# Loads of the first weights moved to another queue, and KV plus W2's first event put side by side, in a gated two-branch attention kernel

## The chip, the cores and the metric

The kernel runs on one core of one Trainium2 chip. The metric is device time in microseconds (us) of one execution. Before the change it is 473.68 us (median of three runs, 473.68 to 473.99).

Names used here: PE is TensorE, PEld its weight loads, ACT is ScalarE, DVE is VectorE, SP is SyncE. "SPq" and "ACTq" lines are DMA issues by those engines. The profiled span is about 1.72 us shorter than the timed value of the same run.

## The reference, cut to what matters

```python
# S = 2048 tokens, D = 1024, 32 heads of 32; x, all weights and the output are bf16
def _A_ref(x, wqkv, wo):                      # linear attention
    q, k, v = split_heads(x @ wqkv)
    phi = lambda t: jnp.where(t > 0, t + 1, jnp.exp(t)) + 1e-6
    pq, pk = phi(q), phi(k)
    kv = jnp.einsum("bhsd,bhse->bhde", pk, v)
    z = jnp.einsum("bhsd->bhd", pk)
    num = jnp.einsum("bhqd,bhde->bhqe", pq, kv)
    den = jnp.einsum("bhqd,bhd->bhq", pq, z)[..., None] + 1e-6
    return merge_heads(num / den) @ wo
# _B_ref: attention of each token to 8 tokens, 2 apart (not touched here)
g = sigmoid((x * gate_w).sum(-1, keepdims=True))
return g * a + (1 - g) * b
```

## The kernel before

Two places matter. The first is the start. K of branch A is projected first: pk = phi(x @ Wk). The contraction over D = 1024 is cut into four pieces k = 0..3 of 256. For each piece the kernel needs x transposed (`xT`, by a transposing DMA) and two halves h of Wk (`WkA[h]`, 256 KB each per piece). TensorE works through piece k with 16 matmuls: eight for half 0 and eight for half 1, over the first four token tiles. While the first data are on their way, 37 matmuls on constants keep TensorE busy, which is meant to bring its clock up early.

```python
    def load_xT(k, t0, t1):
        nc.sync.dma_start_transpose(out=xT[:, 2 * k:2 * k + 2, t0 * P:t1 * P],
                                    in_=rows(x, t0 * P, t1 * P)[:, 2 * k * P:(2 * k + 2) * P])

    def load_wk(eng, k, h):
        eng.dma_start(out=WkA[h][:, 2 * k:2 * k + 2, :], in_=A_wqkv[...])        # 256 KB
    ...
    with tc.manual_schedule(engines={SP, mybir.EngineType.Activation}):
        load_wk(nc.scalar, 0, 0)
        first_act = consts.tile([P, 1], BF16, name="first_act")
        nc.scalar.activation(out=first_act[:], in_=ones[:, 0:1], func=ACT.Exp)
        load_wk(nc.scalar, 0, 1)          # half 1 of piece 0, on ScalarE's queue
        load_xT(0, 0, 2)                  # piece 0 of x, first part (token tiles 0, 1)
        load_xT(0, 2, 4)                  # second part (token tiles 2, 3)
        for k in range(1, 4):
            load_wk(nc.sync, k, 0)
            load_xT(k, 0, 4)
            load_wk(nc.sync, k, 1)
    ...
            warm_up(37)
            for k in range(4):
                for half in range(2):
                    for t in range(4):
                        for kt in (2 * k, 2 * k + 1):
                            project(first[4 * half + t], t, kt, half)
                        ...
```

The second place lies about 116 us in. KV (64-column tiles of the array) is followed by V's projection (full array), into which four "W2 events" are interleaved. Each event multiplies KV into the output weights with sixteen 32x32 tiles of the array at once.

```python
            for g in range(2):
                kvp = ps_1.tile([P, 4, 64], F32, name="kv_ps", tag="p1")
                ...                                            # 64 matmuls
                nc.vector.tensor_copy(out=KVT[:, 4 * g:4 * g + 4, :], in_=kvp[:])
            ...
            def w2_event(g, half):
                def go():
                    w2p = [ps_1.tile([P, 512], F32, name="w2_ps", tag="p1") for _ in range(4)]
                    ...                                        # 16 matmuls, 32x32 tiles, then 4 evacuations
            ...
            units = [u for t in range(4) for u in v_units(t)]
            interleave(units, [(8 + 12 * (2 * g + half), w2_event(g, half)) for g in range(2) for half in range(2)])
```

`ps_1` and `ps_pj` (the projections) have four PSUM banks each.

The softmax here doesn't subtract the row's maximum and nothing guards it: scores larger than these inputs give would overflow.

## Time and profile before

| reading | value |
|---|---|
| time, median | 473.68 us |
| profiled span | 472.3 us |
| PE busy | 466.0 us, 99% |
| PE idle for the first x piece | 0.6 us |
| first real matmul | 5.56 us |
| x's piece k=1 lands | 7.76 us |
| 17th real matmul (the first of piece 1) | 9.42 us |
| clock rises to full | 6.41 us |
| KV's first matmul to the last W2 event | 13.161 us |

The page's first lines and the shares of the chain that ended last (kernel before):

```profile
span 472.3 us, 13144 instructions
...
PE 466.0 (99%) x5734; PEld 244.7 (52%) x5765; DVE 277.4 (59%) x601; ACT 169.1 (36%) x273; POOL 15.4 (3%) x30
...
PE 98%; DMA 1%; issue 0%; ACT 0%
```

TensorE bounds the kernel, and it almost never waits. The list of waits of PE in the kernel before (engine, line and tile, what it waited for, us in total, times, longest):

```profile
PE warm L175 <- PEq L628: 0.8, 1, 0.8
PE pk_ps L169 <- DMA xT<-in_A_x_dram: 0.6, 1, 0.6
PE p_ps L295 <- issue: 0.3, 2, 0.2
```

The start of the kernel before, first PE's timeline, then SyncE's and ScalarE's DMA issues (start, duration, engine, line, operation, tiles, count, idle time before):

```profile
0.84 4.11 PE L175 MATMUL warm<-const-bfloat16-1.0 128*128 128x128 bf16 x37 [0.84 <-PEq L628]
5.56 10.72 PE L169 MATMUL pk_ps<-WkA,xT 128*128 128x512 bf16 x46 [0.61 <-DMA xT<-in_A_x_dram]
...
0.83 0.96 ACTq L98 DMA_DIRECT2D WkA<-in_A_wqkv_dram  x2
...
0.80 2.60 SPq L94 DMA_TRANSPOSE xT<-in_A_x_dram  x2
3.44 0.58 SPq L98 DMA_DIRECT2D WkA<-in_A_wqkv_dram  x1
4.08 1.24 SPq L94 DMA_TRANSPOSE xT<-in_A_x_dram  x1
```

Both halves of the first weights go out on ScalarE's queue at 0.83 to 1.79 us. SyncE issues its two transposes of x at the same time, and each occupies it for about 1.3 us. A matmul of 512 columns starts every 0.216 us at full clock and every 0.43 us before the clock rises.

The same stretch in windows of 1.5 us, kernel before (window, length, busy us of each engine, granted clock, mean busy share of the 16 DMA engines, GB/s; the share can pass 1 because packets overlap):

```profile
2.00:3.50 1.50, 1.50 (x17) 1.50 (x16) 0.00 (x0) 0.28 (x2) 0.00 (x0) 1.00 0.90 232
3.50:5.00 1.50, 1.44 (x14) 1.17 (x11) 0.00 (x0) 0.00 (x0) 0.00 (x0) 1.00 1.16 288
5.00:6.50 1.50, 0.94 (x3) 0.40 (x4) 0.00 (x0) 0.00 (x0) 0.00 (x0) 1.00 1.04 252
```

(The clock column says 1.00 from the beginning; it fills in what has no record. Whether the clock is up is read from the spacing of the matmuls and from the clock records.)

The second place, PE's timeline in the kernel before:

```profile
116.57 2.21 PE L240 MATMUL kv_ps<-G,WvA 128*64 128x64 bf16 x128
118.72 1.90 PE L295 MATMUL p_ps<-WvB,xT 128*128 128x512 bf16 x7
120.55 0.43 PE L283 MATMUL w_ps<-WoA,KVT 32*32 32x512 bf16 x16
120.91 2.76 PE L295 MATMUL p_ps<-WvB,xT 128*128 128x512 bf16 x12
```

A W2 event costs PE 0.46 us: from one V matmul to the next across it 0.677 us pass (120.236 to 120.913), less the usual 0.216.

### The profile page before, as it was taken

The numbers are of one execution on the slowest core, as the hardware profiler recorded it, in microseconds if no ns is written. First come the engines' busy times: TensorE is split into PE (matmuls) and PEld (weight loads), VectorE is DVE, ScalarE is ACT, GpSimd is POOL, SyncE is SP. The second block draws the span as 40 slices with busy tenths as digits, with TensorE's granted clock in tenths as the row PEclk, the third lists the DMA queues.
The fourth block names the chain that finished last, engine by engine and source line by source line (L and its number), as shares of the span: only waits on it lengthen the run. The fifth ranks groups of instructions, "written<-read, shape, count | busy, mean of one in ns | idle before, by whom it ended". The sixth has DMA issues, their size and how long they took to land.

```text
span 472.3 us, 13144 instructions
## 1 busy us (share of the span) xinstructions
PE 466.0 (99%) x5734; PEld 244.7 (52%) x5765; DVE 277.4 (59%) x601; ACT 169.1 (36%) x273; POOL 15.4 (3%) x30
## 2 busy tenths in 40 slices
PE   8999999999999999999999999999999999999997
PEld 5444444445444444445666666666664444444444
DVE  0496689990329999999567676767560049800000
ACT  1343321102443333333555555555551134221122
POOL 3300000500000000000000000000000000000000
PEclk9999999999999999999999999999999999999999
DMA  8999970000634233527326526452563933211001
GB/s 212 212 242 374 348 239 0 0 1 0 203 123 125 95 141 129 156 96 247 107 54 108 105 53 95 100 95 51 92 158 79 196 97 78 71 53 46 34 33 46
DMA packets 98780, 55.40 MB, mean 117 GB/s; under 512 B 70178, under 2 KB 90658, under 8 KB 98722
## 3 DMA queue, kind: packets, MB, share of 16 engines
q1 hardware_dynamic: 93282, 49.84, 41.1%
q10 hardware_dynamic: 5440, 4.72, 3.0%
q8 instruction: 45, 0.74, 0.7%
q14 instruction: 13, 0.11, 0.1%
HBM read 26.10 MB, written 15.86 MB: 89 GB/s over the span
## 4 chain that ended last, share of the span: by engine, by line
PE 98%; DMA 1%; issue 0%; ACT 0%
PE q_ps L388 27%; PE d_ps L585 12%; PE pk_ps L169 12%; PE p_ps L295 12%; PE g_ps L220 12%; PE e_ps L585 11%; PE p_ps L331 9%; PE po L467 2%; PE s2b L445 2%; DMA xT<-in_A_x_dram 1%; PE kv_ps L240 0%; PE w_ps L283 0%; ACT osb L590 0%
## 5 line engine op out<-in xcount | busy, mean ns | idle before, releaser
L388 PE MATMUL q_ps<-xT,WqB 64*64 64x512 bf16 x1024 | 68.3, 377 | 0.0
L388 PE MATMUL q_ps<-xT,WkB 64*64 64x512 bf16 x1024 | 67.9, 377 | 0.0
L156 DVE TENSOR_SCALAR e<-e 128x512 f32<-128x512 f32 x64 | 27.0, 423 | 64.3 <-ACT e L155 64.3
L295 PE MATMUL p_ps<-WvB,xT 128*128 128x512 bf16 x250 | 57.3, 379 | 0.5 <-issue 0.3
L169 PE MATMUL pk_ps<-WkA,xT 128*128 128x512 bf16 x251 | 55.6, 381 | 0.9 <-DMA xT<-in_A_x_dram 0.6
L220 PE MATMUL g_ps<-pk,xrow 128*128 128x512 bf16 x251 | 55.2, 379 | 0.3
L450 ACT ACTIVATE PT<-s2b 128x928 bf16<-128x928 f32 (+4 forms) x40 | 34.2, 854 | 45.5 <-PE s2b L445 45.5
L452 DVE TENSOR_TENSOR PT<-PT,mask 128x928 bf16<-128x928 bf16 (+4 forms) x40 | 23.6, 590 | 38.2 <-ACT PT L450 38.2
L331 PE MATMUL p_ps<-WqA,xT 128*128 128x512 bf16 x187 | 43.1, 379 | 0.3
L585 PEld LDWEIGHTS <-pqT 128*128 128x128 bf16 x272 | 26.0, 98 | 29.8 <-issue 0.4
L585 PEld LDWEIGHTS <-OBT 128*128 128x128 bf16 x272 | 26.0, 98 | 29.3
L169 PEld LDWEIGHTS <-xT 128*128 128x128 bf16 x256 | 25.1, 98 | 31.2 <-DMA xT<-in_A_x_dram 0.9
L220 PEld LDWEIGHTS <-xrow 128*128 128x128 bf16 x256 | 25.0, 98 | 30.2
L295 PEld LDWEIGHTS <-xT 128*128 128x128 bf16 x256 | 24.6, 98 | 30.0 <-issue 0.9
L388 PEld LDWEIGHTS <-WkB 64*64 64x64 bf16 x1024 | 31.7, 107 | 15.4 <-issue 0.4
L388 PEld LDWEIGHTS <-WqB 64*64 64x64 bf16 x1024 | 31.4, 106 | 15.4 <-issue 0.7
L155 ACT ACTIVATE e<-pk_ps 128x512 f32<-128x512 f32 x32 | 18.9, 597 | 40.8 <-PE pk_ps L169 36.6
L300 ACT CAST tmp<-p_ps 128x512 bf16<-128x512 f32 x32 | 18.8, 590 | 37.9 <-PE p_ps L295 29.2
L585 PE MATMUL d_ps<-WoA,pqT 128*128 128x512 bf16 (+1 forms) x133 | 30.7, 369 | 0.2
L585 PE MATMUL d_ps<-WoB,OBT 128*128 128x512 bf16 (+1 forms) x134 | 30.7, 369 | 0.1
L331 PEld LDWEIGHTS <-xT 128*128 128x128 bf16 x192 | 18.8, 98 | 22.7
L585 PE MATMUL e_ps<-WoB,OBT 128*128 128x512 bf16 (+2 forms) x133 | 29.7, 363 | 0.2
(62 smaller groups left out, 484.6 us busy)
## 6 DMA issues: line engine op xcount, KB each, us to landing
vd<-tmp SPq DMA_DIRECT2D x16, 264.0 KB
xrow<-in_A_x_dram SPq DMA_DIRECT2D x4, 1024.0 KB
out_dram<-osb ACTq DMA_DIRECT2D x31, 128.0 KB
pqd<-tmp SPq DMA_DIRECT2D x12, 256.0 KB
WvA<-in_A_wqkv_dram SPq DMA_DIRECT2D x2, 1024.0 KB
WoA<-in_A_wo_dram SPq DMA_DIRECT2D x2, 1024.0 KB
WvB<-in_B_wqkv_dram SPq DMA_DIRECT2D x2, 1024.0 KB
WqA<-in_A_wqkv_dram SPq DMA_DIRECT2D x2, 1024.0 KB
```

The source lines that it names most:

```text
L155: nc.scalar.activation(out=e[:], in_=pj[:], func=ACT.Exp)
L156: nc.vector.tensor_scalar(out=e[:], in0=e[:], scalar1=1.0, scalar2=1e-6, op0=ALU.min, op1=ALU.add)
L169: nc.tensor.matmul(pj[:], lhsT=xT[:, kt, t * P:(t + 1) * P], rhs=WkA[half][:, kt, :], start=(kt == 0), stop=(kt == KT - 1))
L220: nc.tensor.matmul(pj[:], lhsT=xrow[:, t, kt * P:(kt + 1) * P], rhs=pk[:, t, half * 512:(half + 1) * 512], start=(t == 0), stop=(t == NB - 1))
L295: nc.tensor.matmul(st["pj"][:], lhsT=xT[:, kt, t * P:(t + 1) * P], rhs=WvB[half][:, kt, :], start=(kt == 0), stop=(kt == KT - 1))
L300: nc.scalar.copy(out=v[:, half * 16:(half + 1) * 16, 0:Dh], in_=st["pj"][:].rearrange("p (h e) -> p h e", h=16))
L331: nc.tensor.matmul(st["pj"][:], lhsT=xT[:, kt, t * P:(t + 1) * P], rhs=WqA[half][:, kt, :], start=(kt == 0), stop=(kt == KT - 1))
L388: nc.tensor.matmul(banks[o][64 * j:64 * j + 64, :], lhsT=lhsT(r, kt, j), rhs=rhs(r, kt), start=first and kt == 0, stop=kt == KT - 1, skip_ ...
L445: nc.tensor.matmul(s2b[64 * par:64 * par + 64, pair, :, o:o + w], lhsT=kts[c][r, par, k0:k0 + 64], rhs=qz[r, :, par, q0 % 512:q0 % 512 + w ...
L450: nc.scalar.activation(out=pt[:, :, 0:W_], in_=s2b[:].rearrange("p a b s -> p (a b) s")[:, :, 0:W_], func=ACT.Exp, scale=SCALE)
L452: nc.vector.tensor_tensor(out=pt[:, :, 0:W_], in0=pt[:, :, 0:W_], in1=mask[:, None, base:base + W_].broadcast_to([P, 4, W_]), op=ALU.mult)
L585: nc.tensor.matmul(st["ps"][:, 0:n], lhsT=lhsT, rhs=W[c0 // 512][:, c, c0 % 512:c0 % 512 + n], start=(side == 0 and c == 0), stop=(side == ...
```

## The change

Its intent was to get the first x piece to TensorE earlier by taking half 1's weights out of ScalarE's queue, and to save one change of tile shape by putting W2's first event straight behind KV.

```diff
-    with tc.manual_schedule(engines={SP, mybir.EngineType.Activation}):
+    with tc.manual_schedule(engines={SP}):
         load_wk(nc.scalar, 0, 0)
-        first_act = consts.tile([P, 1], BF16, name="first_act")
-        nc.scalar.activation(out=first_act[:], in_=ones[:, 0:1], func=ACT.Exp)
-        load_wk(nc.scalar, 0, 1)
         load_xT(0, 0, 2)
         load_xT(0, 2, 4)
+        load_wk(nc.sync, 0, 1)
         for k in range(1, 4):
             load_wk(nc.sync, k, 0)
             load_xT(k, 0, 4)
...
-                kvp = ps_1.tile([P, 4, 64], F32, name="kv_ps", tag="p1")
+                kvp = ps_pj.tile([P, 512], F32, name="kv_ps", tag="pj")[:, 0:256].rearrange("p (c d) -> p c d", c=4)
...
-                nc.vector.tensor_copy(out=KVT[:, 4 * g:4 * g + 4, :], in_=kvp[:])
+                nc.vector.tensor_copy(out=KVT[:, 4 * g:4 * g + 4, :], in_=kvp)
...
-            interleave(units, [(8 + 12 * (2 * g + half), w2_event(g, half)) for g in range(2) for half in range(2)])
+            w2_event(0, 0)()
+            interleave(units, [(20, w2_event(0, 1)), (32, w2_event(1, 0)), (44, w2_event(1, 1))])
```

## The prediction

> **What bounds it now.** TensorE: the page has PE busy 466.0 of 472.3 us (99%), the chain of waits is 98% PE. The waits view gives PE one wait for another unit: 0.6 us for the first x piece, before the first real matmul. So the change can pay only at the start (0 to 9 us) and where PE changes tile shape (116 to 131 us).
>
> **Start.** By the packet records half 0's weights (256 KB, ScalarE's queue) land at 3.88 us. The first x transpose's packets run from 2.8 to 3.7 us, yet its completion writes go out only at 4.42, when half 1's weights (256 KB, also ScalarE's queue, 3.5 to 4.4 us) are through, and it lands at 5.51. The second x piece's completion writes follow its last packet at once (4.88) and land 0.9 us later. So half 1's weights hold back x by about 0.7 us, and x's second piece too. This agrees with the Trainium skill, "DMA: Bandwidth & Descriptors", section "Issuing engines are not separate DMA queues": both queues share the same 16 engines.
>
> With these weights out of the way I estimate completion writes at 3.75 and landing at 4.65 to 4.75, so that the first matmul follows the last warm-up matmul (start 4.63) without a gap: at 4.75, not 5.56. But the clock rises only at 6.4 us (matmul starts 5.56, 5.96, 6.39, then every 0.216). If it still does, the earlier start wins two slow matmuls: the fifth starts at 6.45 instead of 6.83, a gain of 0.4 us (0.8 if the clock rises earlier too).
>
> Half 1's weights now land at about 6.2 to 6.7 and are needed by the ninth matmul at about 7.3. Later SyncE issues slip by 0.58 us; the slack is larger (x's k=1 piece landed at 7.76, so at most 8.35, needed at 9.0). Dropping the dummy activation (0.20 us) costs nothing: the table load stays, ScalarE idles until 17 us.
>
> **KV and W2.** Each W2 event costs PE 0.46 us (V matmul starts 120.24 to 120.91, less one pitch of 0.216), though its 16 parallel tiles need one pitch: the rest is change of tile shape. The Trainium skill, "TensorEngine Tiling (Array Packing)", "Key Properties", says a mode change drains the engine. With W2's first event behind KV, KV to V (0.13) plus V to W2 (0.09 over a pitch) becomes one KV to W2 change, estimated 0.13: gain 0.1 us. By the build it waits only for the first KV copy, which ends at 118.23, before KV's last matmul at 118.59. KV in the projection banks frees the four W2 banks; without that W2 would wait for KV's second copy (119.25).
>
> **Time.** 473.68 - 0.4 - 0.1 = 473.2 us. Range 472.5 to 473.8. Faster by over 2%: 0.01; within 2%: 0.98; slower by over 2%: 0.01.
>
> **What would show it.** First x piece lands at about 4.7; PE's wait for it vanishes; first real matmul at 4.75, the first four at 0.43 each; the ninth does not wait. V starts at about 119.08 less the start's gain, and KV, W2 and the first eight V matmuls together are 0.1 shorter. Everything later is shifted by 0.5 us.
>
> **What would make it wrong.** Half 1's weights landing after 7.3 us; the clock rising at another phase (0.4 us either way); x's landing bounded by something else; a KV to W2 change as dear as the two it replaces; the timer, whose three readings differ by 0.31 us.

## The result, and the profile after

The changed kernel took 473.73 us (median of 6 runs, 473.44 to 474.22), the kernel before 473.68 (6 runs, 473.36 to 473.99). The ratio is 1.0003 with a 95% interval of 0.999 to 1.0015: no change that the timer resolves. Ratios and intervals here are those over fast runs in the same rounds; they are not quite the ratios of the medians, nor always those of the means of all runs. The forecast gain of 0.5 us did not come.

The page of the changed kernel:

```profile
span 472.5 us, 13174 instructions
...
PE 467.8 (99%) x5765; PEld 246.4 (52%) x5765; DVE 277.2 (59%) x601; ACT 169.2 (36%) x272; POOL 15.3 (3%) x30
...
PE 97%; DMA 1%; SPq 1%; ACT 0%; issue 0%
```

(PE's busy time is higher by 1.8 us, most likely because this trace has 31 more matmul records; a few per cent can be missing. The program has as many matmuls as before.) SPq is new in the chain. The waits of PE in the changed kernel:

```profile
PE pk_ps L167 <- DMA xT<-in_A_x_dram: 0.9, 2, 0.7
PE warm L173 <- PEq L627: 0.8, 1, 0.8
```

The wait for x did not vanish: it went from 0.6 us once to 0.9 us in two places. Where they are is in the timelines of the start, changed kernel, PE first and then the DMA issues:

```profile
0.84 4.11 PE L173 MATMUL warm<-const-bfloat16-1.0 128*128 128x128 bf16 x37 [0.84 <-PEq L627]
4.74 1.10 PE L167 MATMUL pk_ps<-WkA,xT 128*128 128x512 bf16 x4
6.01 2.80 PE L167 MATMUL pk_ps<-WkA,xT 128*128 128x512 bf16 x12 [0.18 <-DMA xT<-in_A_x_dram]
9.51 6.87 PE L167 MATMUL pk_ps<-WkA,xT 128*128 128x512 bf16 x31 [0.69 <-DMA xT<-in_A_x_dram]
...
0.83 0.44 ACTq L98 DMA_DIRECT2D WkA<-in_A_wqkv_dram  x1
...
0.80 2.60 SPq L94 DMA_TRANSPOSE xT<-in_A_x_dram  x2
3.45 1.09 SPq L98 DMA_DIRECT2D WkA<-in_A_wqkv_dram  x2
4.58 1.24 SPq L94 DMA_TRANSPOSE xT<-in_A_x_dram  x1
```

The first matmul starts at 4.74 us, as forecast. But after four matmuls PE waits for x's second part (landed 5.97), and after sixteen it waits for x's piece k=1, which lands at 9.46 us where it landed at 7.76 before. The 17th matmul starts at 9.51 us, after 9.42 before. The 0.8 us won at the first matmul were all given back within sixteen matmuls.

The windows of the changed kernel show what the DMA engines did meanwhile:

```profile
2.00:3.50 1.50, 1.50 (x17) 1.50 (x16) 0.00 (x0) 0.08 (x1) 0.00 (x0) 1.00 0.91 238
3.50:5.00 1.50, 1.50 (x15) 1.34 (x14) 0.00 (x0) 0.00 (x0) 0.00 (x0) 1.00 0.66 125
5.00:6.50 1.50, 1.32 (x7) 0.45 (x6) 0.00 (x0) 0.00 (x0) 0.00 (x0) 1.00 0.91 240
```

From 3.5 to 5 us they moved 125 GB/s in place of 288, at a busy share of 0.66 in place of 1.16. Summed over the packet records, 641 KB had been moved by 5.5 us, and 890 KB in the kernel before. The difference is about the 256 KB of half 1's weights, which ScalarE's queue had brought in by then.

The second place, changed kernel:

```profile
116.66 2.21 PE L238 MATMUL kv_ps<-G,WvA 128*64 128x64 bf16 x128
118.81 0.43 PE L281 MATMUL w_ps<-WoA,KVT 32*32 32x512 bf16 x16
119.18 4.49 PE L293 MATMUL p_ps<-WvB,xT 128*128 128x512 bf16 x20
```

KV to the last W2 event takes 13.054 us, after 13.161: 0.107 us saved, as forecast.

The rest of the span splits cleanly. From the 17th matmul to KV's first matmul both kernels take 107.15 us (to 0.01). Between W2 and the stage of branch B's projections (64x64 tiles) they take the same, and so they do after that stage. In that stage itself the changed kernel took 141.088 us and the kernel before 140.864. So the profiled span of the changed kernel is longer by 0.085 (start) minus 0.107 (W2) plus 0.224 (stage B), together 0.20, against 472.505 less 472.286, 0.22. The 0.22 in stage B are not an effect of the change: the next two profiles of the same changed kernel have 140.884 there. They come from one moment at which the two interleaved row streams of 64x64 matmuls shift against each other (at 352.1 us here, at 304.5 us in w2_only below). It happened in 2 of the 16 profiles. Why it happens is not settled.

### The profile page after: what moved, and what is told of

Same layout as the page of the kernel before. It is cut to its first block, busy times and chain, and to the rows that moved or that the text cites. A ratio compares the mean times of both kernels' runs of the same rounds, so it can differ in the third digit from the quotient of the medians.

```text
span 472.5 us, 13174 instructions
## 1 busy us (share of the span) xinstructions
PE 467.8 (99%) x5765; PEld 246.4 (52%) x5765; DVE 277.2 (59%) x601; ACT 169.2 (36%) x272; POOL 15.3 (3%) x30
## 4 chain that ended last, share of the span: by engine, by line
PE 97%; DMA 1%; SPq 1%; ACT 0%; issue 0%
PE q_ps L387 27%; PE d_ps L584 12%; PE p_ps L293 12%; PE g_ps L218 12%; PE e_ps L584 12%; PE pk_ps L167 11%; PE p_ps L329 9%; PE po L466 2%; PE s2b L444 2%; DMA xT<-in_A_x_dram 1%; SPq L94 1%; PE kv_ps L238 0%; PE w_ps L281 0%; SPq L98 0%; ACT osb L589 0%
## 5 line engine op out<-in xcount | busy, mean ns | idle before, releaser
L584 PE MATMUL e_ps<-WoA,pqT 128*128 128x512 bf16 (+2 forms) x136 | 30.0, 363 | 0.0
```

The lines of the kernel that those rows point to most:

```text
L584: nc.tensor.matmul(st["ps"][:, 0:n], lhsT=lhsT, rhs=W[c0 // 512][:, c, c0 % 512:c0 % 512 + n], start=(side == 0 and c == 0), stop=(side == ...
```

## The experiments

The theory (A): x's piece k=1 is the new limit, because half 1's weights now stand ahead of it in the same queue. Rivals: (B) the slow landing was chance; (C) the moment of the clock's rise, which differs from run to run, hid the gain. Within A there are two versions: A1, DMA engine time was lost while only SyncE's queue fed the engines; A2, only the place in the queue counts, by its issue time or its bytes.

The "17th matmul" of the table is read back from KV's first matmul (107.15 us later in all profiles but one, to 0.01). The exception is h1_two_issues, where the count back gives 9.36, but the 17th matmul itself starts at 8.88; there the 25th then waits for half 1's weights of piece 1 (landed 10.99, PE idle 0.25 us). "Moved" is the sum of the packet records that ended by 5.5 us, rounded down.

| run | first matmul | x k=1 lands | 17th matmul | clock rises | moved by 5.5 us | KV to last W2 | span |
|---|---|---|---|---|---|---|---|
| before | 5.56 | 7.76 | 9.42 | 6.41 | 890 KB | 13.161 | 472.29 |
| changed | 4.74 | 9.46 | 9.51 | 4.88 | 641 | 13.054 | 472.50 |
| same_again | 4.52 | 8.93 | 8.98 | 4.24 | 642 | 13.055 | 471.77 |
| same_again_2 | 4.75 | 8.85 | 8.90 | 4.85 | 636 | 13.054 | 471.69 |
| start_only | 4.77 | 9.14 | 9.20 | 5.71 | 683 | 13.161 | 472.09 |
| w2_only | 5.79 | 7.77 | 9.25 | 4.05 | 844 | 13.054 | 472.31 |
| kv_banks_only | 5.65 | 7.80 | 10.92 | 9.36 | 893 | 13.161 | 473.82 |
| w2_first_old_banks | 5.49 | 7.64 | 9.35 | 6.34 | 919 | 13.639 | 472.70 |
| x1_before_h1 | 4.74 | 6.71 | 10.47 | 6.64 | 653 | 13.055 | 473.25 |
| h1_gated_5 | 4.74 | 8.91 | 9.61 | 4.81 | 687 | 13.055 | 472.39 |
| h1_gated_1 | 4.51 | 9.42 | 12.01 | 4.13 | 605 | 13.055 | 474.81 |
| h1_between | 4.74 | 8.90 | 9.00 | 5.43 | 796 | 13.054 | 471.77 |
| h1_two_issues | 4.65 | 8.83 | 8.88 | 3.54 | 685 | 13.054 | 472.24 |
| h1_half_bytes | 5.29 | 8.40 | 8.82 | 5.47 | 681 | 13.055 | 471.60 |
| x0_whole | 4.75 | 8.58 | 8.63 | 4.80 | 771 | 13.055 | 471.33 |
| x0_whole_2 | 4.81 | 8.69 | 8.74 | 4.08 | 799 | 13.055 | 471.46 |

### same_again and same_again_2: the changed kernel, unchanged

> The changed kernel once more, unchanged. Theory A (x's k=1 piece is now the limit: its issue comes 0.5 us later and it queues behind half 1's weights in the one SyncE queue): it lands again at 9.3 to 9.6 us and the 17th matmul starts right after it at about 9.5, whatever the moment at which the clock rises. Rival B (the slow stretch of the transpose packets at 7.4 to 8.6 us was chance): it lands at about 8.4 and the 17th matmul starts by 9.1. Rival C (only the moment of the clock's rise differs from run to run, and hid the gain): the rise lies elsewhere than 4.88 us and the 17th matmul's start moves with it. Time like before's within 0.1%.

> The changed kernel a third time, beside the two above: x's k=1 piece at 8.9 to 9.5 us, 17th matmul 0.05 us behind it; ratio to before 0.999 to 1.000.

x's piece k=1 landed at 8.93 and 8.85 us, after 9.46 in the first profile: between the 9.3 to 9.6 expected under A and the 8.4 under B. The landing does differ by half a microsecond from run to run, so the first trace showed a bad case. But it never comes near the 8.35 us that the prediction gave as the latest, and the 17th matmul starts 0.05 us behind it in all three profiles. Rival B explains about 0.6 of the 1.7 us, not the rest. Rival C fails for the changed kernel: the clock rose at 4.88, 4.24 and 4.85 us, early each time, and the gain that an early rise should have brought (0.8 us) did not show. Another wait also appears: half 1's weights land at 6.9 to 7.0 and the ninth matmul waits for them. PE's waits in same_again:

```profile
PE pk_ps L167 <- DMA WkA<-in_A_wqkv_dram: 0.5, 1, 0.5
```

Times: 473.51 us (6 runs) against 473.70 before, ratio 0.999 (0.9972 to 1.0008), and 473.45 (5 runs) against 473.58, ratio 1.0002 (0.9988 to 1.0015). Neither interval excludes 1.

### start_only and w2_only: each part alone

The changed kernel with the KV and W2 lines of before, and the kernel before with only those lines changed.

> Only the change of the first loads; KV and W2 as before. Theory A: first matmul at 4.74 us, 17th at about 9.5 behind x's k=1 piece, nothing gained: 473.7 to 473.9 us (ratio 1.000 to 1.001). Rival B or C: 17th at 8.7 to 9.1, 473.2 to 473.4.

> Only KV in the projection banks and W2's first event behind it; first loads as before. All theories: first KV matmul to ninth V matmul takes 4.25 us where the kernel before takes 4.35 (0.09 less), start as before (x's k=1 piece lands at about 7.8, no wait at the 17th matmul). Time 0.1 us below before, which the timer may not resolve (ratio 0.9995 to 1.0005).

The new start alone gives a 17th matmul at 9.20 us, right behind x's piece k=1 (9.14; again between the 9.5 of A and the 8.7 to 9.1 of B or C), and 473.74 us against 473.70, ratio 0.9993 (0.9977 to 1.0009): nothing that the timer resolves. The W2 part alone gives 13.054 us from KV to the last event, 0.107 less than before, and the start is that of before. Its time, 473.90 us (ratio 1.0001, 0.9983 to 1.002), is no lower than before; its profile has the shift in stage B (141.152 against 140.864 us), which hides the 0.107. The effect of the W2 part is therefore taken from the trace, where all profiles with the same order and banks of KV and W2 agree to 0.001 us, and not from the timer.

w2_only also shows what the old start does when the clock rises early (4.05 us): the first matmul starts at 5.79, no later one waits for DMA, and the 17th follows at 9.25. With the late rise of the first profile (6.41) it was 9.42. So the old start at its usual clock ends at 9.25 to 9.42 us (kv_banks_only, 10.92, is left out; see the rare slow executions), and the new one at 8.90 to 9.51. The gain left is 0.1 to 0.3 us on average, with an overlap of the two ranges.

### kv_banks_only and w2_first_old_banks: which half of the W2 part does it

```diff
 kv_banks_only:       KV in ps_pj as in the changed kernel; W2 events at 8, 20, 32, 44 as before
 w2_first_old_banks:  KV in ps_1 as before; W2's first event straight behind KV
```

> The kernel before with KV in the projection banks, W2's first event still after eight V matmuls. First KV matmul to last W2 event's start 13.16 us as before: the banks alone give nothing, the 0.107 us come from the dropped change of tile shape.

> The kernel before with W2's first event straight behind KV, but KV still in W2's own banks. Two of the event's four banks are then KV's, and its third matmul waits for KV's second copy: a stall of about 0.5 us on PE behind KV; first KV matmul to last W2 event's start 13.4 to 13.7 us (before 13.16, with both parts 13.05).

Each was run once, for its trace; the state of a single run is unknown, so only times inside the stage are used. The banks alone change nothing (13.161). The order alone costs 0.48 us (13.639), because two of the event's four banks are still KV's. PE's timeline in w2_first_old_banks:

```profile
118.65 0.39 PE L283 MATMUL w_ps<-WoA,KVT 32*32 32x512 bf16 x3
119.24 0.43 PE L283 MATMUL w_ps<-WoA,KVT 32*32 32x512 bf16 x13 [0.20 <-DVE KVT L242]
```

Three matmuls go (two were expected), then the event waits for DVE's second copy out of KV. Only both together save the 0.107 us.

### x1_before_h1: the queue's order turned round

In the diff the loop's pass for k = 1 is written out; in the kernel the loop runs over k = 2, 3.

```diff
         load_xT(0, 2, 4)
+        load_xT(1, 0, 4)
         load_wk(nc.sync, 0, 1)
         load_wk(nc.sync, 1, 0)
-        load_xT(1, 0, 4)
         load_wk(nc.sync, 1, 1)
```

> The changed kernel with x's k=1 piece issued on SyncE ahead of half 1's first weights (order: x k=0 in two parts, x k=1, half 1 k=0, half 0 k=1, half 1 k=1). Theory A (whichever of these is last holds the matmuls up; the bytes are the same): x's k=1 piece lands at about 7.2, half 1's weights at about 8.2 to 8.6, so the stall moves to the ninth matmul (about 8.4 in place of 7.0), 17th at about 10.1, slower than the changed kernel by 0.6 to 0.9 us. If SyncE's order doesn't matter, nothing moves.

x's piece k=1 lands at 6.71 us, 2.1 to 2.8 us earlier than in the changed kernel, and half 1's weights at 8.71. The stall moves to the ninth matmul. PE's timeline in x1_before_h1:

```profile
4.74 2.83 PE L170 MATMUL pk_ps<-WkA,xT 128*128 128x512 bf16 x8
8.75 3.61 PE L170 MATMUL pk_ps<-WkA,xT 128*128 128x512 bf16 x15 [1.18 <-DMA WkA<-in_A_wqkv_dram]
```

The 17th matmul is at 10.47 us and the time 474.97 us, ratio to before 1.0027 (1.0014 to 1.0039). The direction is that of theory A: the load put behind the other holds the matmuls up. The size is larger than expected (17th at about 10.1, 0.6 to 0.9 us slower than the changed kernel): the median is 1.2 us above that of the changed kernel's first runs (473.73).

### h1_gated_5 and h1_gated_1: half 1's weights on ScalarE's queue, but later

If the old arrangement was only too early, holding half 1's weights back on ScalarE's queue should give both gains. The load is held by activations that write into its tile first.

```diff
         load_wk(nc.scalar, 0, 0)
+        for i in range(5):                       # h1_gated_1: range(1)
+            nc.scalar.activation(out=WkA[1][:, 0, 0:P], in_=ones, func=ACT.Exp)
+        load_wk(nc.scalar, 0, 1)
         load_xT(0, 0, 2)
         load_xT(0, 2, 4)
-        load_wk(nc.sync, 0, 1)
```

> The changed kernel, but half 1's first weights go back to ScalarE's queue, held there by five short activations that write into their tile first (results overwritten by the load), so that they are issued at about 3.4 us instead of 1.35. SyncE's order is that of before. Theory A: first x piece lands at 4.7 as in the changed kernel, half 1's weights at about 6.5, x's k=1 piece at 7.8 to 8.3 as it is issued 0.5 us earlier and shares the engines with a second queue; 17th matmul at 8.4 to 8.9 without a wait for DMA; 0.5 to 0.9 us faster than the changed kernel (ratio to before 0.998 to 0.999). Rival B or C: no better than the changed kernel by more than the clock's moment explains.

> As h1_gated_5 with one activation as the gate in place of five, so that half 1's weights are issued at about 2.4 us and move at about 3.5 to 4.6. Theory A1 (what was lost is engine time: while SyncE issues its transposes, one queue leaves the engines part idle, and in the kernel before half 1's weights from the other queue filled that time): first x piece lands at 4.7 to 4.9, half 1's weights at about 5.5, x's k=1 piece at 7.7 to 8.2 although nothing but the moment of one load differs from h1_gated_5 (8.91); 17th matmul at 8.3 to 9.0, ratio to before 0.998 to 0.9995. Theory A2 (only the place in SyncE's queue counts): x's k=1 piece at about 8.9 as in h1_gated_5, whose SyncE order is the same; ratio 1.000.

Both failed. With five activations the load was issued at 3.79 us (expected 3.4) and landed at 7.83 (expected 6.5), so the ninth matmul waited until 7.88; x's piece k=1 landed at 8.91 although SyncE issued it as early as in the kernel before. Time 474.27 us, ratio 1.0004 (0.9988 to 1.0021). With one activation the load was issued at 2.43 to 2.83, in the middle of SyncE's second transpose (2.15 to 3.39), and both slowed to a trickle: that part of x landed at 7.90, half 1's weights at 7.70. PE stood still for 2.4 us, and its clock fell (records: up at 4.13, down at 7.55, up at 10.96 us). The profile is of the slowest of the five runs (476.52, mean clock 0.996); the others, 474.62 to 475.58 at 0.999 to 1.000, are slow without such a fall. PE's timeline in h1_gated_1:

```profile
4.51 1.04 PE L169 MATMUL pk_ps<-WkA,xT 128*128 128x512 bf16 x4
7.95 6.39 PE L169 MATMUL pk_ps<-WkA,xT 128*128 128x512 bf16 x21 [2.39 <-DMA xT<-in_A_x_dram]
```

Time 475.12 us, ratio 1.0025 (1.0011 to 1.0039). So A1 in the simple form "fill the idle time from the other queue" is not confirmed: from 3.5 to 5 us the engines moved 106 GB/s in h1_gated_1, less even than the 125 of the changed kernel. In the kernel before the same two queues were issued together from 0.8 us and reached 288 GB/s. What makes the difference between those two overlaps is open.

### h1_two_issues and h1_half_bytes: issue time or bytes

h1_two_issues loads half 1's first 256 KB by two loads of 128 KB in place of one. h1_half_bytes makes only the first of these two loads and sets the rest of the tile to zero, so its weights are wrong. Each was timed twice: 473.74 us, ratio 0.9998 (0.9973 to 1.0024), and 472.95 us, ratio 0.9982 (0.9956 to 1.0008).

> The changed kernel with half 1's first 256 KB loaded by two SyncE loads of 128 KB in place of one: one more issue (about 0.5 us), the same bytes. If SyncE's issue time holds x's k=1 piece back: it lands 0.4 to 0.6 us later than in the changed kernel (9.3 to 9.9, changed kernel 8.85 to 9.46 in three profiles). If the bytes ahead of it do: no later than 9.5, within the changed kernel's range.

> The changed kernel with only half of half 1's first weights loaded (128 KB; the rest of the tile is set to zero, so the result is wrong on purpose): as many issues, half the bytes. If the bytes hold x's k=1 piece back (about 300 KB per us moved): it lands at 8.3 to 8.8, about 0.45 us earlier; if issue time does: 8.85 to 9.46 as in the changed kernel.

With one more issue x's piece k=1 was issued 0.45 us later (5.03 against 4.58) and landed at 8.83, no later than in the changed kernel. With half the bytes it landed at 8.40, earlier than in all four profiles of the new start (8.85 to 9.46), though in that run even the first piece landed late (5.24). One profile each, against a scatter of 0.6 us, is not much, but both say the same: bytes ahead of it delay that piece, and one extra issue at that place does not. The packet records agree. In every profile with this order of loads and all bytes, x's piece k=1 lands 0.56 to 0.81 us after the moment at which 1,328 KB have been moved (the five loads of 256 KB up to and with this piece, and 48 KB from before the first of them). That moment is 6.95 to 7.21 us in the four profiles with the old start, and 8.13 to 8.68 in the four of the new.

### h1_between: half 1's weights between the two parts of x's piece 0

```diff
         load_xT(0, 0, 2)
+        load_wk(nc.sync, 0, 1)
         load_xT(0, 2, 4)
-        load_wk(nc.sync, 0, 1)
```

> The changed kernel with half 1's weights on SyncE between the two parts of x's k=0 piece, so that they move while the second part is being issued. Theory A: first part lands at 4.7, half 1's weights at 5.3 to 5.8, second part at 6.0 to 6.4 (fifth matmul waits up to 0.4 us), kilobytes moved by 5.5 us above 750, x's k=1 piece at 8.0 to 8.5 as the engines idle less; 17th matmul at 8.5 to 9.1; 0.2 to 0.6 us faster than the changed kernel. Rival: x's k=1 piece at about 9 as the bytes ahead of it are the same.

The early part came as expected: weights at 5.70, second part of x at 6.36 us, 796 KB moved by 5.5 us. But x's piece k=1 landed at 8.90, no earlier (8.0 to 8.5 was expected; the rival, "at about 9 as the bytes ahead of it are the same", is what came); the 112 to 160 KB won by 5.5 us were lost again by 8.2. The packet records show where: the weights just ahead of that piece took from 5.29 to 7.47 us to move, as late an end as in the new start (7.10 to 7.67). The 17th matmul started at 9.00, the time was 473.69 us, ratio 1.0002 (0.999 to 1.0015). So the kilobytes moved by 5.5 us do not alone decide when piece k=1 lands.

### x0_whole and x0_whole_2: x's piece 0 by one transpose

```diff
-        load_xT(0, 0, 2)
-        load_xT(0, 2, 4)
+        load_xT(0, 0, 4)
         load_wk(nc.sync, 0, 1)
```

> The changed kernel with x's k=0 piece loaded by one transpose in place of two, everything else in the same order. A transpose takes SyncE 1.24 to 1.3 us to issue whatever its size, so all later loads are issued 1.25 us earlier: half 1's weights at 2.2 us, x's k=1 piece at about 3.3 to 4.6. Theory A (SyncE's issue time and the part idle engines behind it hold back x's k=1 piece): first x piece lands at 4.9 to 5.1 (all 256 KB of it), x's k=1 piece at 7.0 to 8.0, 17th matmul at 8.4 to 9.0 without a wait for DMA; kilobytes moved by 5.5 us above 750 (after 641, before 890); 0.3 to 0.8 us faster than the changed kernel. Rival (the queue's bytes alone count): x's k=1 piece still at about 9, no gain.

> x's k=0 piece in one transpose, once more: x's k=1 piece at 8.3 to 8.8 us, 17th matmul at 8.6 to 9.0; span of the profiled run 471.3 to 471.8; ratio to before 0.9985 to 0.9995.

One transpose of 256 KB takes SyncE as long to issue as one of 128 KB (1.34 against 1.30 us), and it lands just as early: at 4.71 us all of it, where in the changed kernel the first half landed at 4.68. Everything behind it is issued 1.25 us earlier. PE's timeline of x0_whole:

```profile
4.75 7.50 PE L166 MATMUL pk_ps<-WkA,xT 128*128 128x512 bf16 x31
```

No matmul of the start waits long enough to be split off, though the ninth starts 0.28 us late, at 6.79, on half 1's weights (landed 6.74); in x0_whole_2 that wait is listed, 0.20 us. The windows of x0_whole:

```profile
3.50:5.00 1.50, 1.50 (x16) 1.31 (x14) 0.00 (x0) 0.00 (x0) 0.00 (x0) 1.00 0.92 162
5.00:6.50 1.50, 1.50 (x8) 0.68 (x7) 0.00 (x0) 0.00 (x0) 0.00 (x0) 1.00 1.12 310
```

The engines moved 162 GB/s from 3.5 to 5 us and 310 from 5 to 6.5, where the changed kernel had 125 and 240. x's piece k=1 landed at 8.58 and 8.69 (expected 7.0 to 8.0, missed; the rival said about 9), and the 17th matmul started at 8.63 and 8.74 us, the earliest of all full-data kernels here. That is 0.5 to 0.8 us earlier than with the old start at its usual clock (9.25 to 9.42), and 0.2 to 0.9 us earlier than the changed kernel. Times: 473.45 us (5 runs) against 473.58, ratio 0.9997 (0.9984 to 1.0009), and 473.41 (6 runs) against 473.53, ratio 0.999 (0.9975 to 1.0006). It is the best version by its traces, but the timer does not tell it from the kernel before. Neither version of theory A is enough alone: x1_before_h1 and h1_half_bytes speak for the bytes ahead in the queue (A2), and x0_whole, with the same bytes in the same order and a landing 0.2 to 0.9 us earlier than in the changed kernel, for engine time lost behind SyncE's long issues (A1).

### The rare slow executions

Of 47 timed runs of the kernel before, four took 475.6 to 475.8 us; the other 43 stayed at or below 474.4. One of the six runs of w2_only (475.43) and the one run of kv_banks_only (475.56) look the same, and all of these have the old start. kv_banks_only was profiled in such a run. Its clock rose only at 9.36 us, nine of its first sixteen matmuls ran at the slow pace, and the 17th started at 10.92 us. Its PE shows a gap of 0.70 us before the first matmul:

```profile
5.65 8.68 PE L169 MATMUL pk_ps<-WkA,xT 128*128 128x512 bf16 x30 [0.70 <-DMA xT<-in_A_x_dram]
```

The kernels whose profiles go from the warm-up to the first real matmul without a gap, or with one of at most 0.28 us (changed kernel, same_again, same_again_2, start_only, h1_between, both x0_whole, h1_two_issues, and h1_gated_5 in spite of its later wait of 1.21 us; 47 timed runs together) have nothing above 474.58. Two others without the gap, x1_before_h1 and h1_gated_1, took 474.62 to 476.52, but in them the later stall is part of the time. The Trainium skill, "TensorE: Matmul & The Clock Gate", section "What's actually happening", says that the clock is set by how busy PE was in a window of 3.4 us that runs freely and does not begin with the kernel. The fall and rise in h1_gated_1 lie 3.41 us apart and agree. The window that ended 3.41 us before the late rise, from 2.54 to 5.95 us, holds the whole gap. That the gap kept the clock down is thus a likely reading of one trace, not a shown one: the kernel before in its first profile had a gap of 0.61 us, and its clock rose at 6.41, at the end of a window (3.0 to 6.41) that held it too.

## Why the prediction was right or wrong

- **What bounds the kernel, and where the change can act**: right. All differences lie in the first sixteen matmuls, in the 13 us around W2, and in the chance shift of stage B.
- **Half 1's weights held back the first x piece**: right. It lands at 4.42 to 4.73 us in place of 5.45 to 5.75 (5.51 in the first profile), and the first matmul starts at 4.52 to 4.77 where 4.75 was forecast.
- **The clock rises at 6.4 us, so only 0.4 us are won**: not a fixed moment. It rose at 3.5 to 9.4 us in these sixteen profiles. This did not decide the result: in four profiles of the new start it rose at 4.2 to 5.7, which by the prediction should have given up to 0.8 us.
- **"Half 1's weights now land at about 6.2 to 6.7"**: too early. They landed at 6.89 to 7.29 us, and in three of the four profiles of the new start the ninth matmul waited for them (until 6.96 to 7.34).
- **"Later SyncE issues slip by 0.58 us; the slack is larger (x's k=1 piece landed at 7.76, so at most 8.35, needed at 9.0)"**: this is the step that failed. The issue slipped by 0.50 us, as said, but the landing slipped by 1.1 to 1.7 us, to 8.85 to 9.46. I treated a load as something that lands a fixed time after its issue. By the packet records it lands 0.6 to 0.8 us after its own bytes and all those ahead of it have been moved, and 256 KB that used to move mostly from 3.5 to 4.5 us, while SyncE was issuing transposes, now moved afterwards. The busy share of the DMA engines in that slot fell from 1.16 to 0.66 (288 to 125 GB/s). x's packets (256 bytes each, the weights' 1,024) show the step itself. On average over the four profiles of each start, the first packet of piece k=1 starts 0.59 us later, which is about the forecast slip of the issue; but its packets then take 2.0 us in place of 1.25. In 11 of the 15 profiles with weights just ahead of it in the queue, its last packet ends 0.91 to 0.94 us after the last packet of those weights (in the other four 1.04 to 1.80; the 1.80 is the first profile of the changed kernel), and those weights end at 7.10 to 7.67 us in the four new starts, at 6.20 to 6.36 in the four old ones. The late bytes are not all of it: an estimate from these records is 235 KB at 280 KB per us, 0.84 of the 1.26 us by which the moment of 1,328 KB moved. The rest is slower moving: from 5.5 us to that moment the old starts moved 275 to 283 KB per us, the new ones 216 to 261. Why is open. The Trainium skill, "DMA: Bandwidth & Descriptors", section "Issuing engines are not separate DMA queues", which I had quoted, also says that issuing from several engines saves only issue time, which is usually small beside the transfer. For transposes the trace shows more: 1.24 to 1.3 us of issue each, and x's first two parts, whose packets took 0.8 to 1.8 us each in the new start, left the engines part idle.
- **KV and W2 save 0.1 us**: right, 0.107 us in each profile. It agrees with the Trainium skill, "TensorEngine Tiling (Array Packing)", section "Key Properties": a change of mode drains the engine, and one change less is what was saved; no record shows the draining itself. In the kernel before, the 0.46 us of the first event split into one pitch, 0.05 us in which its sixteen matmuls start, and 0.09 and 0.10 us above a pitch at the two changes. The remark that W2 would wait for KV's second copy without the new banks was right too (0.48 us).
- **The time**: 473.2 forecast, 473.73 measured at first; all 17 timed runs of the changed kernel have a median of 473.53 and the 47 of the kernel before 473.68. That 473.73 lies inside the forecast range says little, since the range also held no change at all. The term that was mis-sized is the start: 0.4 us forecast; measured at the 17th matmul, the four new starts average 9.15 us and the three old ones with a usual clock 9.34, so about 0.2 us, less than the timer resolves. (That is (9.51 + 8.98 + 8.90 + 9.20) / 4 and (9.42 + 9.25 + 9.35) / 3.)

What stays open: why the new starts and h1_between moved their bytes more slowly after 5.5 us (199 KB per us in h1_between), why the two queues fed the engines well from 0.8 us on but badly when the second was issued at 2.4, how much idle time keeps the clock down, and what makes the row streams of stage B slip.

## What to carry to other kernels

Before moving a load out of the way of another, look at what the DMA engines do in its time slot: where the moved load was filling that slot, as here, its bytes only move to a later place, and the stall moves to whatever now stands behind them. Follow the loads up to the point where compute has real slack again, not only to the first matmul. If SyncE's transposes take as long to issue as to transfer, merging two of them won more here, by the traces, than reordering the copies around them.

## What the Trainium skill lacked or had wrong

- "DMA: Bandwidth & Descriptors", "Issuing engines are not separate DMA queues": the issue time that several issuing engines save, called usually small there, was not small for transposes. Those of pieces 0 and 1 took SyncE 1.21 to 1.35 us each to issue (one of piece 2, in h1_gated_1, 2.20), and the DMA engines' busy share from 3.5 to 5 us fell from 1.16 to 0.66 when the other queue's copy was taken away.
- The same page does not say, for this chip, how the issue time of a transpose goes with its size: 1.30 us for 128 KB and 1.34 us for 256 KB here.
- The same page says that transposes and plain copies of two queues need no care beside each other. For correctness no run contradicts it, but where a copy was issued on ScalarE's queue during a transpose's issue on SyncE, both were slow: the part of x that lands at 5.1 to 6.0 us in the new start landed at 7.9 (h1_gated_1).
- "TensorE: Matmul & The Clock Gate" does not say how much idle time within a window keeps the clock down. With a gap of 0.70 us the clock rose at 9.36 us, with one of 0.61 us at 6.41; in h1_gated_1 it fell at 7.55, with 2.0 us of a 2.4 us gap before that moment.
- "TensorEngine Tiling (Array Packing)" gives no cost of a mode change: one change less saved 0.107 us. No page tells of the slip between the row streams of 64x64 tiles that cost 0.22 to 0.29 us in 2 of 16 profiles.
